# Two 64-token tiles, one batch's loads and a table of conversion steps moved in a fused attention and MLP kernel

## The chip, the cores and the metric

The kernel runs on one core of one Trainium2 chip. The metric is the device time of one execution in microseconds (us); for the kernel before, three runs gave 1006.35, 1006.38 and 1009.82 us, a median of 1006.38 us. The profile is of one more execution, on the same core. Engines are named as in the profile: PE is TensorE, DVE is VectorE, ACT is ScalarE, POOL is GpSimd, and SP is the engine whose queue issues the DMAs.

## The reference

Eight batches of eight heads, 576 tokens, head size 64. Keys and values are averaged over groups of 8 tokens, so each query sees 72 keys. The result goes through an MLP with a leaky ReLU.

```python
k_p = k.reshape(B, H, Sp, pool, D).mean(axis=3)        # 576 -> 72 rows
v_p = v.reshape(B, H, Sp, pool, D).mean(axis=3)
scores = scale * np.matmul(q, k_p.transpose(0, 1, 3, 2))
scores = scores - np.max(scores, axis=-1, keepdims=True)
attn = np.exp(scores)
attn = attn / (np.sum(attn, axis=-1, keepdims=True) + 1e-09)
x = np.matmul(attn, v_p)       # then [B*S, 512] = [4608, 512]
h = x @ w_in                   # [4608, 2048]
g = np.maximum(0.01 * h, h)
out = g @ w_out                # [4608, 512]
```

## The kernel before

**The MLP.** The 4608 tokens are cut into nine chunks of 512. Chunk 0 holds tokens 0 to 511 of batch 0, chunk 1 those of batch 1; the last 64 tokens of both batches wait in a tile `x_tail` and become the first 128 tokens of chunk 2. The hidden size of 2048 is cut into 16 slices f of 128. For one chunk and one slice, `m1` multiplies x by `w_in` (12 matmuls of 512 columns, into a tile `ph`; x and the weight are each split into a high and a low part, and three of the four products are made), ACT applies the leaky ReLU and splits off the high part `gh`, DVE makes the low part `gl`, and `m2` multiplies these by `w_out` (12 matmuls into four accumulators). `m2` runs two slices behind `m1`. The order of the (chunk, slice) pairs is a list of runs (L645): first chunk 0 with slices 0 to 7, then chunk 1 with all 16, then chunk 0 with slices 8 to 15, then chunks 2 to 8. The half-finished chunk 0 is stored in DRAM between the first and the third run.

**The weights.** Each slice of `w_in` and `w_out` arrives as raw 64-bit numbers (`stage`, four slices ahead) and is converted into a high and a low 32-bit part in two steps, a head and a tail (`convert`): two ACT and three DVE instructions (L183 to L189), then one ACT and one DVE instruction (L193, L194). There are 32 conversions, so 64 steps, in the order of `steps`; `convert_to(n)` issues all steps below n. A head or a tail of a given conversion is therefore placed by the calls of `convert_to` and by the letter `c` in the string `FIRST`, each of which is one step.

**The attention.** Work of one tile of (at most) 128 tokens is cut into units: `q` (PE transposes of q into `pq`, ACT copy to `qT`), `sa` (scores into `pss` for four heads, DVE maximum L401, ACT exponential L403), `sb` (sum and reciprocal on DVE, normalised `at` on POOL, or on DVE for tiles 2 and 3 of batch 0), `pu` (PE transposes of `at` into `pp`, ACT and DVE split them into `pT_hi`, `pT_lo`, `pT_rem`), and `au` (16 matmuls of the attention with the pooled values into `pa`, two halves per piece, ACT and DVE split the result into `xh` and `xl`, or DVE copies it into `x_tail`, L488). `ku` and `vu` put the pooled keys and values in place; `lk` and `lv` do the pooling, on DVE for most of batch 0 and on POOL for the others. `PIECES` says which tiles share one `au`.

**The order.** On PE the order is the order in which the code issues (`manual_schedule`, L750). On the other engines a scheduler decides, and `order` below lists what it decided. The opening is the string `FIRST`: the attention of batch 0 with 14 conversion steps strewn in. After it, the units of batch 1 (and the string `TAIL_STEPS`) are spread evenly between the halves of `m1` and `m2` of the first run (L806 to L822); those of batches 2 to 7 stand in the later runs. While batch 0 is worked on, PSUM tiles rotate through eight banks (`banks`, L202); from the `/` in `FIRST` on, attention units have two banks in turn.

**Borrowed space.** `spare(f, i, ...)` hands out the space of a converted weight of a late slice f before that weight exists. Raw k and v of batches 0 and 1 (`RAW`, L213), the wide `at` and `e` tiles and the second set of `pT` tiles (`piece_tiles`, L430) live there. A tile that takes over such a place waits until the last reader of the one before is done.

The functions that the change touches and their callers:

Of the kernel before, what the change touches and what calls it, by code (L numbers as in the profile page):

```python
# [10 lines left out]
F32 = mybir.dt.float32  # L11
# [13 lines left out]
def tile_pooled_attention_ffn(  # L25
# [11 lines left out]
    P = 128  # L37
# [19 lines left out]
        [[(0, 128), (128, 128)], [(256, 128), (384, 128)], [(512, 64)]],  # L57
        WHOLE,
        [[(0, 128), (128, 128)], [(256, 128)], [(384, 128), (512, 64)]],
# [4 lines left out]
    FIRST = (  # L64
# [3 lines left out]
    )  # L68
    TAIL_STEPS = "pu40 au20 pu41 au21"
    SPLIT = 8  # L70
# [133 lines left out]
    turn = 0  # L204

    def bank(b, name):
        nonlocal turn
        pool, tag = banks[turn % len(banks)] if b == 0 else banks[0]
        turn += 1
        return pool.tile([P, NK, P], F32, tag=tag, name=name)  # L210


    RAW = {  # L213
        (0, "k0"): (10, 0), (0, "k1"): (10, 1), (0, "v0"): (11, 0), (0, "v1"): (11, 1),
        (0, "krem"): (9, 0), (0, "vrem"): (9, 1),
        (1, "k0"): (4, 0), (1, "k1"): (4, 1), (1, "v0"): (5, 0), (1, "v1"): (5, 1),
    }
# [94 lines left out]
    tiles = [[x for piece in p for x in piece] for p in PIECES]  # L312
    every = [(b, t) for b in range(B) for t in range(len(tiles[b]))]

    def load_q(b, t):
        s0, n = tiles[b][t]
        if b == 0:
            qr = one.tile([P, H, D], F32, tag=f"xh1_{t}" if t < NK else "xl1_0", name=f"q{b}_{t}")
        else:
            qr = two.tile([P, H, D], F32, tag="q", name=f"q{b}_{t}")  # L320
        nc.sync.dma_start(qr[:n], q[b, :, s0 : s0 + n, :].rearrange("h s d -> s h d"))
        return qr

# [106 lines left out]
    def piece_tiles(b, j, g):  # L430
        if b > 0 or g == 0 or j == 2:
            return pT
        return {
            part: spare(10 - n // 2, n % 2, t.shape, F32R, f"pT_{part}{b}_{j}_{g}")
            for n, (part, t) in enumerate(pT.items())
# [20 lines left out]
    def av_unit(b, j, g, pc):  # L456
        s0 = PIECES[b][j][0][0]
        n = sum(n for _, n in PIECES[b][j])
        w = max(n, PMIN) if b > 0 else n
        for i in range(2):  # L460
# [53 lines left out]
    def attention(b):  # L514
# [5 lines left out]
        def loads():  # L520
# [4 lines left out]
            start_v()  # L525
            for t in range(2, 5):
                q_of[b, t] = load_q(b, t)
# [225 lines left out]
    att[0]["loads"]()  # L753
    stage(0)
    stage(1)
    att[1]["loads"]()
    for f in range(2, SPARE):
        stage(f)

    for u in FIRST.split():  # L760
        if u == "c":
            convert_to(stepped + 1)
        elif u == "/":
            del banks[1:]
            turn = 0
        else:
            att[0][u]()
    att[1]["lk"]()
    att[1]["lv"]()
# [28 lines left out]
    for n, (c, fs) in enumerate(runs):  # L798
# [63 lines left out]
```

## Time and profile before

| | before |
|---|---|
| median of three runs | 1006.38 us |
| span of the profiled execution | 1006.5 us |
| PE busy | 954.4 us (95%) |
| DVE busy | 370.1 us (37%) |
| ACT busy | 428.4 us (43%) |
| POOL busy | 177.7 us (18%) |

The span of the profiled execution, from its first to its last instruction, is 1006.5 us, and no other time of that execution is given; it lies 0.1 us from the median. A start time in the rows is counted from the span's start. Matmul ends in the profile are modelled and overlap the next matmul's start, so the time that a matmul costs is read from one start to the next. A wait in brackets behind a row is the idle time of that engine just before the row, and the instruction that ended it.

### The profile page before, as it was taken

The page shows a single profiled execution, that of the slowest core. Times are in us where ns is not written, and L with a number is a line of the kernel's source. Part 1 is how long each engine was busy: PE and PEld are TensorE (multiplying, and loading weights), DVE is VectorE, ACT ScalarE, POOL GpSimd, SP SyncE. Part 2 cuts the span into 40 slices and gives each one's busy share as a digit, 9 for nine tenths or more (in the row PEclk, how much of TensorE's full clock was granted, in tenths as well). Part 3 has the DMA queues.
Part 4 walks back from the last instruction along what each step waited for, and adds up shares of the span by engine and source line. Part 5 has one row for each costly group of instructions (what it writes and reads, how often), then busy time and mean ns, then how long its engine had stood idle before and what let it go on. Part 6 is the DMA issues. An engine that isn't in the chain of part 4 may idle for free.

```text
span 1006.5 us, 12735 instructions
## 1 busy us (share of the span) xinstructions
PE 954.4 (95%) x4536; PEld 779.0 (77%) x4536; DVE 370.1 (37%) x902; ACT 428.4 (43%) x1386; POOL 177.7 (18%) x292
## 2 busy tenths in 40 slices
PE   4478999999999999999999999999999999999998
PEld 3357778878787778878888888788877888788886
DVE  5998639223432322332232333243323332221111
ACT  5678657234433343424353434344433433332121
POOL 3602200401116610133013301230110100000000
PEclk9679999999999999999999999999999999999999
DMA  9954311312034400221022202110100010001001
GB/s 246 268 170 142 94 54 42 93 43 69 1 102 102 105 11 12 63 71 35 6 64 58 58 1 69 37 37 1 58 22 1 11 48 1 1 1 42 0 1 42
DMA packets 65582, 57.44 MB, mean 57 GB/s; under 512 B 39920, under 2 KB 49136, under 8 KB 65520
## 3 DMA queue, kind: packets, MB, share of 16 engines
q1 hardware_dynamic: 64944, 56.11, 19.8%
q8 instruction: 36, 0.59, 0.2%
q10 hardware_dynamic: 576, 0.52, 0.2%
q14 instruction: 26, 0.21, 0.1%
HBM read 46.14 MB, written 10.49 MB: 56 GB/s over the span
## 4 chain that ended last, share of the span: by engine, by line
PE 79%; DVE 7%; ACT 4%; DMA 4%; issue 2%; POOL 2%; SPq 1%; ACTq 0%; DVEq 0%; POOLq 0%
PE ph L661 12%; PE acc L685 12%; PE ph L663 11%; PE ph L662 11%; PE acc L687 11%; PE acc L686 11%; PE pss L393 4%; PE pp L442 2%; PE pq L368 1%; ACT e L403 1%; DVE w_t L186 1%; DMA v0raw<-in_v_dram 1%; DVE w L194 1%; DVE w_t L189 1%; SPq L240 1%
## 5 line engine op out<-in xcount | busy, mean ns | idle before, releaser
L661 PE MATMUL ph<-xh,w 128*128 128x512 f32 x576 | 237.2, 412 | 1.0 <-DVE gl L670 1.0
L685 PE MATMUL acc<-w,gh 128*128 128x512 f32 x576 | 233.1, 405 | 0.0
L663 PE MATMUL ph<-xh,w 128*128 128x512 f32 x576 | 227.5, 395 | 0.0
L662 PE MATMUL ph<-xl,w 128*128 128x512 f32 x576 | 227.1, 394 | 0.0
L687 PE MATMUL acc<-w,gl 128*128 128x512 f32 x576 | 225.5, 391 | 0.0
L686 PE MATMUL acc<-w,gh 128*128 128x512 f32 x576 | 225.2, 391 | 0.0
L670 DVE TENSOR_TENSOR gl<-ph,gh 128x512 fp32r<-128x512 f32 x144 | 99.5, 691 | 264.6 <-ACT gh L669 263.8
L666 ACT ACTIVATE ph<-ph 128x512 f32<-128x512 f32 x144 | 84.2, 585 | 253.2 <-PE ph L663 253.0
L403 ACT ACTIVATE e<-pss,red 128x72 f32<-128x72 f32 (+1 forms) x320 | 98.2, 320 | 116.9 <-DVE red L401 116.6
L417 POOL TENSOR_TENSOR at<-e,red 128x256 f32<-128x256 f32 (+1 forms) x76 | 47.5, 624 | 543.5 <-DVE red L415 294.7
L663 PEld LDWEIGHTS ph<-xh,w 128*128 128x128 f32 x576 | 109.3, 190 | 24.3
L661 PEld LDWEIGHTS ph<-xh,w 128*128 128x128 f32 x576 | 109.4, 190 | 23.3 <-DVE gl L670 1.5
L687 PEld LDWEIGHTS acc<-w,gl 128*128 128x128 f32 x576 | 108.3, 188 | 23.9
L685 PEld LDWEIGHTS acc<-w,gh 128*128 128x128 f32 x576 | 108.2, 188 | 22.0 <-issue 1.6
L662 PEld LDWEIGHTS ph<-xl,w 128*128 128x128 f32 x576 | 109.7, 190 | 19.2
L686 PEld LDWEIGHTS acc<-w,gh 128*128 128x128 f32 x576 | 108.4, 188 | 19.6
L669 ACT CAST gh<-ph 128x512 fp32r<-128x512 f32 x144 | 85.4, 593 | 3.1
L401 DVE TENSOR_REDUCE red<-pss 128x4 f32<-128x288 f32 (+1 forms) x80 | 36.1, 454 | 95.2 <-PE pss L393 94.3
L403 ACT ACTIVATION_READ_ACCUMULATOR e<-pss,red 128x1 f32 (+1 forms) x320 | 65.4, 204 | 0.0
L393 PEld LDWEIGHTS pss<-kT,qT 128*128 128x128 f32 (+1 forms) x320 | 47.9, 186 | 15.3 <-ACT qT L370 5.8
L393 PE MATMUL pss<-kT,qT 128*128 128x144 f32 (+1 forms) x320 | 54.7, 298 | 4.5 <-ACT qT L370 4.5
L448 DVE TENSOR_TENSOR pT_lo<-pp,pT_hi 128x256 fp32r<-128x256 f32 (+1 forms) x80 | 31.7, 396 | 68.1 <-ACT pT_rem L445 67.5
(95 smaller groups left out, 840.9 us busy)
## 6 DMA issues: line engine op xcount, KB each, us to landing
q<-in_q_dram SPq DMA_DIRECT2D x32, 256.0 KB, 4.3
w_bits<-in_moe_w_in_dram SPq DMA_DIRECT2D x16, 512.0 KB, 3.7
w_bits<-in_moe_w_out_dram SPq DMA_DIRECT2D x16, 512.0 KB, 3.3
out_dram<-o SPq DMA_DIRECT2D x31, 256.0 KB, 2.7
k0raw<-in_k_dram SPq DMA_DIRECT2D x16, 256.0 KB, 3.6
k1raw<-in_k_dram SPq DMA_DIRECT2D x16, 256.0 KB, 4.3
v0raw<-in_v_dram SPq DMA_DIRECT2D x16, 256.0 KB, 4.2
v1raw<-in_v_dram SPq DMA_DIRECT2D x16, 256.0 KB, 5.2
```

The lines of the kernel that those rows point to most:

```text
L393: nc.tensor.matmul(sc[:n, 2 * SP * i : 2 * SP * (i + 1)], qT[:, p, :n], kT[:, p, :, :].rearrange("d i s -> d (i s)"), start=True, stop=True,)
L403: ins = nc.scalar.activation(e[:n, h, :], scv[:n, h, :], AF.Exp, bias=mx[:n, h : h + 1], accum_out=sm[:n, h : h + 1],)
L417: eng.tensor_tensor(at[:n, 0:2, :].rearrange("a i (h s) -> a (i h) s", h=2), e[:n, :, 0:MAIN], sm[:n].unsqueeze(2).broadcast_to([n, 4, MAI ...
L661: nc.tensor.matmul(ph, w[:, 0, ks], xh[kk], start=kk == 0, stop=False)
L662: nc.tensor.matmul(ph, w[:, 0, ks], xl[kk], start=False, stop=False)
L663: nc.tensor.matmul(ph, w[:, 1, ks], xh[kk], start=False, stop=kk == NK - 1)
L666: nc.scalar.activation(ph, ph, AF.Prelu, alpha=0.01)
L669: casts.append(nc.scalar.copy(gh, ph))
L670: nc.vector.tensor_tensor(gl, ph, gh.bitcast(F32), op=ALU.subtract)
L685: nc.tensor.matmul(a, gh[:, r], hi, start=first, stop=False)
L686: nc.tensor.matmul(a, gh[:, r], lo, start=False, stop=False)
L687: nc.tensor.matmul(a, gl[:, r], hi, start=False, stop=last)
```

## The change

The diff, cut to its core:

```diff
     PIECES = [
         [[(0, 128), (128, 128)], [(256, 128), (384, 128)], [(512, 64)]],
-        WHOLE,
+        [[(0, 128), (128, 128)], [(256, 128), (384, 128)], [(512, 64)]],
...
     FIRST = (
-        "lk ku q0 q1 sa00 sb00 sa01 sb01 lv sa10 sb10 sa11 sb11 q2 sa20 sa21 vu pu00 pu10 c c q3 "
-        "pu01 pu11 c sb20 sb21 au00 sa30 sa31 c au01 c pu20 pu21 sb30 sb31 c c pu30 pu31 c au10 au11 "
-        "c q4 c c / sa40 sa41 sb40 sb41 c c c"
+        "lk ku q0 q1 sa00 sb00 sa01 sb01 lv sa10 sb10 sa11 sb11 q2 sa20 sa21 vu pu00 pu10 q3 "
+        "pu01 pu11 sb20 sb21 au00 sa30 sa31 c c au01 pu20 pu21 sb30 sb31 pu30 pu31 c au10 au11 c c"
     )
-    TAIL_STEPS = "pu40 au20 pu41 au21"
+    TAILS = (
+        "0q4 0sa40 0sa41 1q4 0sb40 0sb41 1sa40 1sa41 0pu40 0au20 0pu41 0au21 "
+        "1sb40 1sb41 1pu40 1au20 1pu41 1au21"
+    )
...
+    first_v = spare(11, 0, [P, 2, NK, 2, D], F32R, "v_first")
+    first = (
+        spare(11, 1, [P, NK, 2, SP], F32, "kT_first"), first_v[:, 0], first_v[:, 1],
+        spare(10, 0, [P, 2, 4, D], F32R, "v_rem_first"),
+    )
+    nc.gpsimd.memset(first[0], 0.0)
+    nc.gpsimd.memset(first_v.bitcast(F32), 0.0)
+
+    def keys_values(b):
+        return first if b == 0 else (kT, v_hi, v_lo, v_rem)
...
-        (0, "k0"): (10, 0), (0, "k1"): (10, 1), (0, "v0"): (11, 0), (0, "v1"): (11, 1),
+        (0, "k0"): (4, 0), (0, "k1"): (4, 1), (0, "v0"): (5, 0), (0, "v1"): (5, 1),
         (0, "krem"): (9, 0), (0, "vrem"): (9, 1),
-        (1, "k0"): (4, 0), (1, "k1"): (4, 1), (1, "v0"): (5, 0), (1, "v1"): (5, 1),
+        (1, "k0"): (9, 0), (1, "k1"): (9, 1), (1, "v0"): (10, 1), (1, "v1"): (8, 0),
...
-            part: spare(10 - n // 2, n % 2, t.shape, F32R, f"pT_{part}{b}_{j}_{g}")
+            part: spare(9 + n // 2, (n + n // 2) % 2, t.shape, F32R, f"pT_{part}{b}_{j}_{g}")
...
-        w = max(n, PMIN) if b > 0 else n
+        w = max(n, PMIN) if b > 1 else n
...
     att[0]["loads"]()
-    stage(0)
-    stage(1)
-    att[1]["loads"]()
-    for f in range(2, SPARE):
+    for f in range(SPARE):
         stage(f)
...
+    del banks[1:]
+    turn = 0
+    att[1]["loads"]()
     att[1]["lk"]()
     att[1]["lv"]()
...
-        if n == 0:
-            us = [att[0][u] for u in TAIL_STEPS.split()] + us
+        if n == 1:
+            us = [att[int(u[0])][u[1:]] for u in TAILS.split()] + us
...
-        beats, done, beat = 4 * len(fs), 0, 0
+        beats, done, beat = (24 if n == 1 else 4 * len(fs)), 0, 0
         for f in fs:
             if n == 0:
-                convert_to(14 + 2.8 * f)
+                convert_to(6 + 4 * f)
             elif n == 1:
-                convert_to(36 + 3 * f)
+                convert_to(36 + 2.2 * f)
```

In words: the 64-token tiles of batches 0 and 1 (tile 4) leave the opening and the first run and stand in the second run, spread over its first 20 beats; a beat is half of an `m1` or `m2`. Batch 0 gets its own place for pooled keys and values, so that they are still there then. `FIRST` holds 5 conversion steps in place of 14. The loads of k and v of batch 1 are issued after `FIRST`, into places that batch 0's attention uses until its end. The q tiles of the two small tiles are loaded later as well.

On PE, around the first product (`ph_0` is the first `m1`, `pk` and `pkr` hold the transposed pooled keys of batch 1, `pa_1_3` is the last attention product of batch 0's tiles 0 to 3). Before:

```order
L470 MATMUL pa_1_3_546<-pT_rem_1_1_475,v_rem 128x256
L368 MATMUL pq_4_559<-ident,q_4_148 128x64 x4
L393 MATMUL pss_4_0_577<-kT,qT_4_564 64x144 x2
L393 MATMUL pss_4_1_587<-kT,qT_4_564 64x144 x2
L661 MATMUL ph_0_645<-xh_0_402,w_0_344 128x512
```

Of the change:

```order
L488 MATMUL pa_1_3_502<-pT_rem_1_1_445,v_rem_first 128x256
L679 MATMUL ph_0_567<-xh_0_371,w_0_407 128x512
L680 MATMUL ph_0_567<-xl_0_375,w_0_407 128x512
L681 MATMUL ph_0_567<-xh_0_371,w_0_407 128x512
L679 MATMUL ph_0_567<-xh_1_372,w_0_407 128x512
L680 MATMUL ph_0_567<-xl_1_376,w_0_407 128x512
L681 MATMUL ph_0_567<-xh_1_372,w_0_407 128x512
L342 MATMUL pk_574<-ident,ksum_522 128x128 x4
L346 MATMUL pkr_581<-ident,kremsum_523 128x64
```

The small tile's `pq` and `pss` are gone from here, and `pk` of batch 1, which stood behind two whole `m1`, stands in the middle of the first.

On SP, whose queue issues the DMAs in this order, around batch 1's k and v; the brackets name the engines and the earlier DMAs that an issue waits for. Before:

```order
L165 DMA w_bits_156<-in_moe_w_out_dram 128x1024 [waits DMAHW2_49]
L240 DMA k0raw_162<-in_k_dram 64x2x512 [waits DMAHW3_49]
L240 DMA k0raw_162<-in_k_dram 64x2x512 [waits DMAHW4_49]
L240 DMA k1raw_165<-in_k_dram 64x2x512 [waits DMAHW5_49]
L240 DMA k1raw_165<-in_k_dram 64x2x512 [waits DMAHW6_49]
```

Of the change:

```order
L253 DMA v1raw_537<-in_v_dram 64x2x512 [waits DMAHW3_49]
L163 DMA w_bits_518<-in_moe_w_in_dram 128x4x256 [waits DMAHW4_49,DVE_49,Activation_49]
L163 DMA w_bits_1686<-in_moe_w_in_dram 128x4x256 [waits DMAHW5_49,DMAHW0_49,Pool_49]
L167 DMA w_bits_1688<-in_moe_w_out_dram 128x1024 [waits DMAHW6_49,DMAHW1_49,Pool_49]
L167 DMA w_bits_520<-in_moe_w_out_dram 128x1024 [waits DMAHW7_49,DVE_49,Activation_49]
L253 DMA k1raw_529<-in_k_dram 64x2x512 [waits DVE_49,PE_49]
L253 DMA k0raw_526<-in_k_dram 64x2x512 [waits PE_49,Activation_49]
L253 DMA k0raw_526<-in_k_dram 64x2x512 [waits DMAHW2_49]
L253 DMA k1raw_529<-in_k_dram 64x2x512 [waits DMAHW3_49]
L253 DMA v0raw_534<-in_v_dram 64x2x512 [waits DMAHW4_49,DVE_49,PE_49]
```

Batch 1's k, which waited for nothing but earlier transfers, now waits for PE (the last matmul that reads the second set of `pT` tiles, whose place it takes) and stands behind four weight loads.

On DVE, in the opening (`pT_lo`, `pT_rem` and `xl` belong to the attention of batch 0, `w_t` and `w` to the conversions). Before:

```order
L452 SCALAR_TENSOR_TENSOR pT_rem<-pp_1_0_336,marks,pT_rem 128x128
L185 TENSOR_SCALAR w_t_345<-w_bits_150 128x512
L185 TENSOR_SCALAR w_t_352<-w_bits_152 128x512
L186 SCALAR_TENSOR_TENSOR w_t_345<-w_bits_150,w_t_345 128x512
L186 SCALAR_TENSOR_TENSOR w_t_352<-w_bits_152,w_t_352 128x512
L189 ISA w_t_345<-w_bits_150,w_t_345 128x1024
L448 TENSOR_TENSOR pT_lo_0_1_368<-pp_0_1_370,pT_hi_0_1_367 128x2x128
```

Of the change:

```order
L469 SCALAR_TENSOR_TENSOR pT_rem<-pp_1_0_321,marks,pT_rem 128x128
L465 TENSOR_TENSOR pT_lo_0_1_339<-pp_0_1_341,pT_hi_0_1_338 128x2x128
L469 SCALAR_TENSOR_TENSOR pT_rem_0_1_340<-pp_0_1_341,marks,pT_rem_0_1_340 128x128
L465 TENSOR_TENSOR pT_lo_0_1_339<-pp_1_1_349,pT_hi_0_1_338 128x2x128
L469 SCALAR_TENSOR_TENSOR pT_rem_0_1_340<-pp_1_1_349,marks,pT_rem_0_1_340 128x128
L503 TENSOR_TENSOR xl_0_375<-pa_0_0_366,xh_0_371 128x256
L503 TENSOR_TENSOR xl_1_376<-pa_0_1_381,xh_1_372 128x256
```

The first conversions no longer stand between the attention instructions here; they start 16 rows further down, behind the normalisation of tile 3.

## Rows read from the trace of the kernel before

**Rows 1.** The page, part 2: the span in 40 equal slices of 25.2 us; busy tenths of PE, and the granted PE clock in tenths of full speed (9 and above is the level of 2.4 GHz, 5 that of 1.2 GHz).

```profile
PE   4478999999999999999999999999999999999998
PEclk9679999999999999999999999999999999999999
```

**Rows 2.** Busy time by stretch. Columns: stretch in us, its length, then busy us and instructions of PE, PE's weight loads, DVE, ACT and POOL, then the granted clock, the DMA share and GB/s. The stretches end at the first matmul of batch 0's values stage, at the end of its attention without the small tile, at the first product, at the third `m1`, at the first product of the second run, at the end of that run, and at the end.

```profile
0.00:22.30 22.30, 8.75 (x42) 7.01 (x42) 11.72 (x40) 9.88 (x44) 8.96 (x22) 0.96 0.93 245
22.30:50.61 28.31, 13.87 (x74) 11.60 (x74) 27.98 (x59) 20.13 (x73) 15.52 (x18) 0.68 0.98 268
50.61:52.77 2.16, 1.70 (x13) 1.33 (x13) 2.16 (x7) 0.75 (x2) 0.00 (x0) 0.90 0.84 339
52.77:73.50 20.73, 14.53 (x57) 11.13 (x56) 18.67 (x43) 16.81 (x47) 2.45 (x4) 0.75 0.46 139
73.50:134.17 60.67, 53.15 (x270) 42.06 (x268) 42.91 (x106) 44.76 (x154) 11.37 (x20) 0.97 0.38 111
134.17:222.00 87.83, 86.78 (x384) 71.56 (x383) 41.46 (x79) 39.96 (x76) 13.75 (x18) 1.00 0.22 64
222.00:1006.50 784.50, 775.59 (x3710) 634.29 (x3708) 225.21 (x572) 296.10 (x993) 125.62 (x210) 1.00 0.13 36
```

**Rows 3.** Timeline of PE in the opening: start, length (us), engine, line, operation, tiles, shape, count, and in brackets the wait before it.

```profile
33.05 0.38 PE L468 MATMUL pa<-pT_lo,v_hi 128*128 128x256 f32 x1 [3.46 <-DVE pT_lo L448]
...
43.29 0.90 PE L442 MATMUL pp<-ident,at 128*128 128x128 f32 x3 [7.79 <-DVE at L417]
...
50.17 0.41 PE L470 MATMUL pa<-pT_rem,v_rem 128*128 128x256 f32 x1
50.51 0.67 PE L368 MATMUL pq<-ident,q 64*128 64x64 f32 x4
...
52.77 0.50 PE L661 MATMUL ph<-xh,w 128*128 128x512 f32 x1
```

**Rows 4.** Timeline of DVE in the opening, same columns.

```profile
27.50 2.36 DVE L186 SCALAR_TENSOR_TENSOR w_t<-w_bits,w_t 128x512 int32<-128x512 int32 x2
29.78 1.21 DVE L189 CUSTOM_DVE_ANT_0 w_t<-w_bits,w_t 128x1024 uint16<-128x1024 uint16 x1
...
34.57 2.45 DVE L194 TENSOR_TENSOR w<-w_t,w 128x512 fp32r<-128x512 f32 x2
36.94 4.12 DVE L414 TENSOR_SCALAR red<-red 128x4 f32<-128x4 f32 x1
...
48.33 0.41 DVE L185 TENSOR_SCALAR w_t<-w_bits 128x512 int32<-128x512 int32 x1
48.67 0.68 DVE L189 CUSTOM_DVE_ANT_0 w_t<-w_bits,w_t 128x1024 uint16<-128x1024 uint16 x1
49.27 0.68 DVE L194 TENSOR_TENSOR w<-w_t,w 128x512 fp32r<-128x512 f32 x1
```

**Rows 5.** Timeline of POOL, same columns: the first and the last instruction of the pooling of batch 1's k and v (18 in all), and two of batch 2's.

```profile
27.69 2.75 POOL L228 TENSOR_TENSOR k0raw<-k0raw 128x512 f32<-128x512 f32 x2 [5.48 <-DMA k0raw<-in_k_dram]
...
42.91 0.49 POOL L234 TENSOR_TENSOR vremsum<-vremraw 64x64 f32<-64x64 f32 x1
...
179.67 2.48 POOL L228 TENSOR_TENSOR k0raw<-k0raw 128x512 f32<-128x512 f32 x2 [53.98 <-DMA k0raw<-in_k_dram]
182.23 0.73 POOL L234 TENSOR_TENSOR ksum<-k0raw 128x256 f32<-128x256 f32 x1
183.70 1.29 POOL L228 TENSOR_TENSOR k1raw<-k1raw 128x512 f32<-128x512 f32 x1 [0.73 <-DMA k1raw<-in_k_dram]
```

**Rows 6.** Timeline of SP's queue: the two issues of batch 1's first half of k.

```profile
17.36 1.25 SPq L240 DMA_DIRECT2D k0raw<-in_k_dram  x2
```

**Rows 7.** The chain that ended last, in order of time: the transfer of batch 2's k, alone on the queues.

```profile
175.54 3.97 DMA k0raw<-in_k_dram
```

**Rows 8.** Timeline of PE from the first product to the third `m1`.

```profile
57.17 0.63 PE L442 MATMUL pp<-ident,at 64*128 64x64 f32 x3 [2.74 <-POOL at L417]
...
63.92 0.37 PE L442 MATMUL pp<-ident,at 64*128 64x64 f32 x3 [1.25 <-DVE x_tail L488]
...
70.83 0.94 PE L327 MATMUL pk<-ident,ksum 128*128 128x128 f32 x4
...
73.50 0.47 PE L661 MATMUL ph<-xh,w 128*128 128x512 f32 x1
```

**Rows 9.** Waits of PE from 73.5 to 134.17 us: who waited for whom, us in total, times, longest.

```profile
PE pq L368 <- ACT e L403: 2.6, 2, 2.1
PE pp L442 <- DVE x_tail L488: 1.8, 1, 1.8
```

**Rows 10.** Timeline of PE: pieces of the two small tiles.

```profile
62.06 0.28 PE L467 MATMUL pa<-pT_hi,v_hi 128*128 128x64 f32 x1
...
62.39 0.28 PE L470 MATMUL pa<-pT_rem,v_rem 128*128 128x64 f32 x1
...
111.34 0.46 PE L368 MATMUL pq<-ident,q 64*128 64x64 f32 x4 [2.09 <-ACT e L403]
...
116.79 0.70 PE L393 MATMUL pss<-kT,qT 128*64 128x144 f32 x4
117.42 0.50 PE L685 MATMUL acc<-w,gh 128*128 128x512 f32 x1
...
123.36 0.37 PE L442 MATMUL pp<-ident,at 64*128 64x64 f32 x3 [0.31 <-DVE pT_rem L452]
123.66 0.50 PE L661 MATMUL ph<-xh,w 128*128 128x512 f32 x1
```

**Rows 11.** Timeline of ACT: the four instructions of two conversion heads end where the second row starts.

```profile
62.09 0.70 ACT L183 ACTIVATE w_bits<-w_bits 128x512 f32<-128x512 f32 x1
...
64.32 0.62 ACT L193 CAST w<-w_t 128x512 fp32r<-128x512 f32 x1
```

More of the change, by code (lines that the diff above doesn't have):

```diff
@@ L312, in tile_pooled_attention_ffn @@
     tiles = [[x for piece in p for x in piece] for p in PIECES]
-    every = [(b, t) for b in range(B) for t in range(len(tiles[b]))]
+    every = [(b, t) for b in range(2) for t in range(4)] + [(0, 4), (1, 4)]
+    every += [(b, t) for b in range(2, B) for t in range(len(tiles[b]))]
     def load_q(b, t):
         s0, n = tiles[b][t]
-        if b == 0:
-            qr = one.tile([P, H, D], F32, tag=f"xh1_{t}" if t < NK else "xl1_0", name=f"q{b}_{t}")
+        if b == 0 and t < NK:
+            qr = one.tile([P, H, D], F32, tag=f"xh1_{t}", name=f"q{b}_{t}")
         else:
@@ L324, in place_k @@
     def place_k(b, sums, rem):
+        kT = keys_values(b)[0]
         pk = bank(b, f"pk{b}")
@@ L338, in place_v @@
     def place_v(b, sums, rem):
+        _, v_hi, v_lo, v_rem = keys_values(b)
         for i in range(2):
@@ L388, in s_unit @@
         n = tiles[b][t][1]
+        kT = keys_values(b)[0]
         pss = bank(b, f"pss{b}_{t}_{g}")
@@ L458, in av_unit @@
         n = sum(n for _, n in PIECES[b][j])
-        w = max(n, PMIN) if b > 0 else n
+        w = max(n, PMIN) if b > 1 else n
+        _, v_hi, v_lo, v_rem = keys_values(b)
         for i in range(2):
@@ L525, in loads @@
             start_v()
-            for t in range(2, 5):
+            for t in range(2, NK):
                 q_of[b, t] = load_q(b, t)
@@ L762, in tile_pooled_attention_ffn @@
             convert_to(stepped + 1)
-        elif u == "/":
-            del banks[1:]
-            turn = 0
         else:
             att[0][u]()
+    del banks[1:]
+    turn = 0
+    att[1]["loads"]()
     att[1]["lk"]()
```

## The prediction

> **What bounds the kernel now.** I read the page's slices first, then busy time by stretch, then the timelines of the first 140 us, and last the waits of PE. The slices show PE at nine tenths or more from the fourth slice on, and a granted clock below full only in the first three [rows 1]. The stretches say where the time that can be saved lies. The second run takes 87.83 us for 384 matmuls, 0.229 us each at the full clock with nothing between them, and the 784 us behind it are 99% busy [rows 2]. Whatever is added there is paid in full. Before the second run, at 134.17 us, PE is not full: 14 of 28 us in the opening's second part, 14.5 of 20.7 us around the first two `m1`, 53 of 61 us in the rest of the first run [rows 2]. In the opening DVE is the bound: busy 27.98 of 28.31 us [rows 2], and PE's long waits there, 3.46 and 7.79 us, end on DVE [rows 3]. After 73.5 us no engine is full: PE 53, DVE 43 and ACT 45 of 61 us [rows 2]; what is lost goes into short waits from engine to engine, 2.6 and 1.8 us the largest [rows 9].
>
> So the sum has two sides: how much earlier the second run begins than at 134.17 us, and how much longer it gets. Durations come from an execution of 1006.5 us, 0.1 us above the median of the three runs, so no correction is made.
>
> **The opening: from 50.5 us to about 44.** Between the first conversion and the last split of `pT` (48.3 us) DVE did 4 instructions of L185, 4 of L186, 3 of L189 and 2 of L194; of the change two each of the first three and none of L194. From start to start L185 takes 0.34 us, L189 0.60 us [rows 4], and I take 0.60 for the other two, which are listed with similar lengths when nothing disturbs them. Removed: 2 x 0.34 + 5 x 0.60 = 3.7 us. Second, DVE was slowed while POOL pooled batch 1 (27.69 to 43.4 us [rows 5]): L186 took 2.36 us for two, L189 1.21, L194 2.45 for two, and a tiny L414 4.12 us [rows 4]. Against 0.68 apiece and about 0.2 for the small one this is 1.0 + 0.5 + 1.1 + 3.9 = 6.5 us. Of POOL's 18 instructions nine (both remainders and half of v) still fall into the opening, the shorter ones; I leave 2.5 us of the 6.5, which removes 4. New is that DVE waits for the exponentials of tile 3, 1 to 2 us that conversions used to fill. 48.3 - 3.7 - 4 + 1.5 = 42.1, and the last eight `pa` matmuls follow at half clock (0.21 us each, as at 50.17 us [rows 3]): 44. Bounds: 41 if POOL disturbs nothing, 48.5 if it disturbs as much as before.
>
> The weights' transfers move ahead of batch 1's; I cost that at nothing, since the first conversion now starts later, at some 32 us. The extra memsets on POOL stand in its idle time before 12 us.
>
> **The new wait: batch 1's keys.** Before, they were pooled while DVE held the opening up anyway, and PE took them at 70.83 us without a wait [rows 8]. Now their transfer can be issued only when the last `pa` has read the `pT` tiles, at 44 us. Four issues of 0.6 us [rows 6], the first landing 4 us after its issue when alone on the queues [rows 7], and I take 4.5 with the weight loads ahead of it; then POOL's adds until the second half of the sum: three long ones at 1.3 to 1.7 us and five at 0.74 us [rows 5], 7.9 us. So `pk` starts at 44 + 0.7 + 4.5 + 7.9 = 57 us. In between PE does half an `m1`: `xl` is ready at 47 to 48 us, six matmuls at half clock (0.43 us) take 2.6 us, and PE then waits about 7 us. Queued behind it are the second half of `m1`, and through it everything of the first run. DVE and ACT go on converting meanwhile, DVE disturbed by the pooling.
>
> Behind `pk` comes ACT: the copy `qT` for batch 1's first tile stands behind a conversion tail that waits for DVE. DVE has some 20 instructions (10.9 us) from 47.5 us to there, plus 3.8 us of disturbance: 62.2; then tail, `gh`, four head instructions in 2.23 us [rows 11] and the copy: 66 us. The third `m1` starts at about 67.5 us, against 73.50 [rows 8]: 6 us gained, half of which is the small tile's units and the two waits behind them, 2.74 and 1.25 us [rows 8].
>
> A rule of the Trainium skill speaks against this wait. The trace shows it first: behind the 7.79 us wait [rows 3] the granted clock of that part of the opening is 0.68 on average, and 0.75 around the first `m1` [rows 2]. The page "TensorE: Matmul & The Clock Gate", section "HAM oscillation — how this bites in real kernels", says that a PE that idles between bursts is throttled again and starts each burst at half rate. By that rule the 18 matmuls behind `pk` cost 0.43 us instead of 0.23, 3.6 us more. In my sum it costs nothing up to 66 us, since the copy on ACT comes later either way; the trace agrees with the rule but makes it matter only for the slower rival.
>
> **The rest of the first run: from 60.7 us to 54.5.** Taken out: batch 1's small tile. From rows at full clock [rows 10]: `pq` 0.4, two `pss` of 0.63, two `pp` of 0.30, and its 64 columns in sixteen wide `pa` 0.5: 2.8 us; and one `pss` of 0.4 now lies earlier. Its two waits (2.09 before `pq`, 1.8 behind the `x_tail` copies [rows 9, 10]) go with it. Added: `pss` of tile 2 now stands directly ahead of `pa`, which needs its PSUM bank, and ACT reaches that exponential only behind four head instructions: about 3 us. Conversions: the change arrives with three conversions (6.5 us of DVE) fewer done, but without the small tiles' work; DVE and ACT each have about 45 us of work in 54, as full as PE. 60.7 - 2.8 - 0.4 - 3.9 + 3 = 56.6, less 2 us of half clock that followed the 2.09 us wait: 54.5. Bounds: 50 (as full as PE was at 90 to 108 us) and 60 (nothing saved but the small tile).
>
> The second run then starts at 67.5 + 54.5 = 122 us: 12.2 us earlier.
>
> **The second run: 9.2 us longer.** Both small tiles now stand where PE is full. Each costs 0.4 + 2 x 0.63 + 2 x 0.30 + 16 x 0.11 = 4.0 us [rows 10], since batch 1's own `pa` no longer shares columns: 8.0 us. The beats leave six matmuls or 1.4 us between a unit and the one that needs it; ACT and DVE queue their own work there, so I add 1.2 us of short waits (bounds 0 and 4). Fewer conversion steps per slice (2.2 for 3) cost nothing: all 64 are issued by slice 13, and DVE is busy 41 of 88 us [rows 2].
>
> **Sum:** 1006.5 - 12.2 + 9.2 = 1003.5; I say 1003 us.
>
> **Rivals.**
> The first run flows. If POOL hardly disturbs DVE and the conversions keep ahead, `pk` comes at 54 and the second run at 116 us: 1006.5 - 18.2 + 9 = 997.5. For it: all three engines then have slack of 10 us each. Against it: DVE was 99% busy in the opening, and no stretch before 134 us ran that full on PE.
>
> The keys come late. The transfers of k stand behind four weight loads of 512 KB, some of which are issued only when DVE and POOL are through; if those are still moving, k lands after 52 us, POOL and DVE disturb each other for longer, and `pk` comes at 64 us. PE then takes the 18 matmuls at half clock (3.6 us), ACT's copy is no cover any more, the third `m1` starts at 75 us, and the second run at 130: 1006.5 - 4.2 + 9.5 = 1012. It decides from `pk` later than about 61 us: there the gain before the second run falls under the 9 us added to it. For it: the queues move 268 GB/s with a share of 0.98 up to 50 us [rows 2]. Against it: a load needs 4 us alone.
>
> The work only changes place. The gain before the second run is eaten by the new wait, and the small tiles cost what they cost before: 1006.5. For it: PE must do all of this work anyway, plus sixteen matmuls.
>
> **How the numbers follow.** This kernel's runs tell 0.5%, 5 us, from no change. Forecast (1003, own range 999 to 1007): 0.47, of which a quarter lies below 1001.4. Free flow (994 to 1001): 0.27. No gain: 0.06. Late keys (1009 to 1017): 0.20, two thirds of it above 1011.4. Faster: 0.27 + 0.12 = 0.39; slower: 0.13; same: the rest, 0.48. The range that holds 8 in 10 takes in most of the free flow and the start of the late keys: 995 to 1010.
>
> **What would show it.** In the changed profile: no instruction of 4 us on DVE before 42 us; the first product at 46 to 48 us; a wait of about 7 us of PE for `ksum` in its middle; the third `m1` at 66 to 69 us; the second run's first matmul at 120 to 124 us; 8 to 10 us more between it and the third run's. It would be wrong if `pk` waits beyond 61 us, if PE in the first run waits for weights instead of ACT and DVE, or if the small tiles hold PE up for more than 4 us in the second run.

## The result, and the profile after

The changed kernel takes 1013.39 us (median of four runs, 1012.12 to 1015.22), the kernel before 1006.37 us beside it: a ratio of 1.0067, 95% interval 1.0048 to 1.0086. It is slower by 7 us. The forecast was 1003 us with a range of 995 to 1010; the time lies above it, and to a time above 1011.4 us the prediction had given 0.13. Of four runs of a later repeat (e8 below) the one that was profiled took 1096.15 us at a granted clock of 0.837, and the ratio and the median of e8 leave it out.

The profiled execution of the change has a span of 1011.4 us, 4.9 us more than before, and took 1013.22 us: 1.8 us lie around the span. The prediction took the span of before, 1006.5 us, for a time; with the same 1.8 us (1.7 to 1.9 in every run whose span and time are both known) that execution took some 1008.3 us (an estimate), 2 us over its median. So profile against profile shows 4.9 us and the medians 7.0.

The page's slices after, for [rows 1]:

```profile
PE   4547999999999999999999999999999999999998
PEclk9769999999999999999999999999999999999999
```

The third and fourth slices, 50.6 to 101.1 us, lost a part: PE was at 7 and 8 tenths there and is at 4 and 7. Busy time by stretch, for [rows 2], cut at the end of batch 0's attention, at the third `m1`, at the second run's first product, and at `pk` of batch 2, which stands at the same place of the third run in both kernels (columns as in [rows 2]). Before, for the last two stretches:

```profile
134.17:226.64 92.47, 91.42 (x404) 75.33 (x403) 41.49 (x79) 41.10 (x78) 13.75 (x18) 1.00 0.20 60
226.64:1006.50 779.86, 770.95 (x3689) 630.52 (x3687) 225.18 (x571) 294.96 (x992) 125.62 (x210) 1.00 0.13 36
```

After:

```profile
22.60:45.01 22.41, 13.58 (x73) 12.29 (x73) 20.70 (x52) 20.88 (x75) 6.76 (x10) 0.66 0.69 225
45.01:74.45 29.44, 11.73 (x39) 7.69 (x38) 19.95 (x41) 10.46 (x26) 13.56 (x9) 0.65 0.63 187
74.45:129.20 54.75, 48.20 (x245) 39.62 (x244) 40.99 (x96) 42.17 (x134) 10.09 (x16) 0.97 0.41 124
129.20:230.94 101.74, 101.74 (x472) 81.65 (x471) 49.13 (x105) 49.30 (x123) 21.07 (x26) 1.00 0.21 60
230.94:1011.40 780.46, 770.85 (x3689) 630.50 (x3687) 224.71 (x571) 294.62 (x992) 125.28 (x210) 1.00 0.13 36
```

The second run begins 134.17 - 129.20 = 4.97 us earlier, takes 101.74 - 92.47 = 9.27 us longer, and the rest 0.60 us: 4.9 in sum. The stretch that stands out is the second one: 29.44 us in which PE works 11.73 and ACT 10.46. The timeline of PE (columns as in [rows 3], with which it compares, and [rows 8]) shows where:

```profile
44.90 0.28 PE L488 MATMUL pa<-pT_rem,v_rem_first 128*128 128x256 f32 x1
45.01 0.42 PE L679 MATMUL ph<-xh,w 128*128 128x512 f32 x1
48.34 0.79 PE L680 MATMUL ph<-xl,w 128*128 128x512 f32 x1 [2.90 <-DVE xl L503]
...
62.89 0.69 PE L342 MATMUL pk<-ident,ksum 128*128 128x128 f32 x2 [12.05 <-POOL ksum L247]
64.25 0.69 PE L342 MATMUL pk<-ident,ksum 128*128 128x128 f32 x2 [0.68 <-POOL ksum L247]
...
74.45 0.40 PE L679 MATMUL ph<-xh,w 128*128 128x512 f32 x1
...
98.81 0.39 PE L485 MATMUL pa<-pT_hi,v_hi 128*128 128x256 f32 x1 [3.61 <-ACT e L420]
```

Half an `m1` is done by 50.6 us, and PE then waits 12.05 us for the pooled keys. The timeline of POOL, for [rows 5], says why:

```profile
51.05 7.31 POOL L241 TENSOR_TENSOR k0raw<-k0raw 128x512 f32<-128x512 f32 x1 [11.80 <-DVE w_t L188]
58.32 1.25 POOL L241 TENSOR_TENSOR k1raw<-k1raw 128x512 f32<-128x512 f32 x1
...
63.48 0.72 POOL L247 TENSOR_TENSOR ksum<-k1raw 128x256 f32<-128x256 f32 x1
```

The same add takes 7.31 us on k0 and 1.25 us on k1. DVE meanwhile (timeline, for [rows 4]):

```profile
51.34 0.41 DVE L187 TENSOR_SCALAR w_t<-w_bits 128x512 int32<-128x512 int32 x1
51.67 0.68 DVE L191 CUSTOM_DVE_ANT_0 w_t<-w_bits,w_t 128x1024 uint16<-128x1024 uint16 x1
...
56.56 0.68 DVE L188 SCALAR_TENSOR_TENSOR w_t<-w_bits,w_t 128x512 int32<-128x512 int32 x1
65.09 0.87 DVE L358 SCALAR_TENSOR_TENSOR v_lo<-vsum,v_hi 64x256 fp32r<-64x256 f32 x2 [7.86 <-ACT v_hi L357]
```

From 51.34 to 57.24 us DVE runs eleven conversion instructions with no gap, each at its undisturbed length (0.68 us for L191, against 1.21 beside POOL's adds in [rows 4]). The add ends at 58.36, 1.1 us after DVE falls idle. Then DVE stands still for 7.86 us: the next in its queue is the placing of v, which waits for ACT's copy, and that for POOL's sum of v (timeline of ACT):

```profile
64.64 0.85 ACT L357 ACTIVATE v_hi<-vsum 64x256 fp32r<-64x256 f32 x2 [8.90 <-POOL vsum L247]
...
68.13 0.58 ACT L684 ACTIVATE ph<-ph 128x512 f32<-128x512 f32 x1 [1.63 <-PE ph L681]
```

So one add that made no headway holds up PE, ACT and DVE together.

### The profile page after: what moved, and what is told of

It is laid out like the page before. It is cut to its first block, busy times and chain, and to the rows that moved or that the text cites. A ratio compares the mean times of both kernels' runs of the same rounds, so it can differ in the third digit from the quotient of the medians.

```text
span 1011.4 us, 12771 instructions
## 1 busy us (share of the span) xinstructions
PE 955.0 (94%) x4552; PEld 778.9 (77%) x4552; DVE 368.3 (36%) x902; ACT 427.2 (42%) x1386; POOL 187.0 (18%) x294
## 4 chain that ended last, share of the span: by engine, by line
PE 88%; ACT 4%; DMA 2%; issue 2%; DVE 2%; POOL 1%; SPq 1%; ACTq 0%; POOLq 0%; DVEq 0%
PE acc L703 13%; PE ph L679 13%; PE acc L705 13%; PE acc L704 13%; PE ph L681 12%; PE ph L680 12%; PE pss L410 4%; PE pp L459 3%; PE pq L384 1%; ACT e L420 1%; SPq L253 1%; PE pa L486 1%; PE pa L488 1%; PE pa L487 1%; PE pa L485 1%
## 5 line engine op out<-in xcount | busy, mean ns | idle before, releaser
L434 POOL TENSOR_TENSOR at<-e,red 128x256 f32<-128x256 f32 (+1 forms) x76 | 51.5, 677 | 537.1 <-DVE red L432 281.9
L410 PEld LDWEIGHTS pss<-kT,qT 128*128 128x128 f32 (+1 forms) x280 | 41.1, 180 | 12.7 <-ACT qT L386 3.4
L410 PE MATMUL pss<-kT,qT 128*128 128x144 f32 (+1 forms) x280 | 46.9, 290 | 2.8 <-ACT qT L386 2.8
```

What stands on the lines that cost most here:

```text
L410: nc.tensor.matmul(sc[:n, 2 * SP * i : 2 * SP * (i + 1)], qT[:, p, :n], kT[:, p, :, :].rearrange("d i s -> d (i s)"), start=True, stop=True,)
L434: eng.tensor_tensor(at[:n, 0:2, :].rearrange("a i (h s) -> a (i h) s", h=2), e[:n, :, 0:MAIN], sm[:n].unsqueeze(2).broadcast_to([n, 4, MAI ...
```

## The experiments

Theory A: GpSimd's add is held up by VectorE's gapless conversions. Rivals: B, the keys' transfers are late; C, ACT and DVE stand behind the placing of v, so that early keys alone bring little. All ratios are to the kernel before, measured beside the run. The kernel before gave medians of 1005.44 to 1007.87 us beside the experiments, so the times below compare by their ratios and not as they stand. One table first, of the profiled executions, in us; "second run" is its first product, "length" goes from there to `pk` of batch 2:

| run | time | ratio (95%) | last `pa` from | third `m1` | second run | length |
|---|---|---|---|---|---|---|
| before | 1006.37 | | 50.17 | 73.50 | 134.17 | 92.47 |
| changed | 1013.39 | 1.0067 (1.0048 to 1.0086) | 44.90 | 74.45 | 129.20 | 101.74 |
| e1 | 1008.95 | 1.0022 (1.0006 to 1.0037) | 44.54 | 66.42 | 125.80 | 101.71 |
| e2 | 1014.65 | 1.0059 (1.0036 to 1.0083) | 42.67 | 71.06 | 130.77 | 101.72 |
| e3 | 1005.90 | 0.9975 (0.9962 to 0.9988) | 42.81 | 65.06 | 121.86 | 101.75 |
| e4 | 1007.44 | 0.9997 (0.9984 to 1.0009) | 43.62 | 63.06 | 122.91 | 101.96 |
| e5 | 1003.38 | 0.9974 (0.9963 to 0.9985) | 42.68 | 65.18 | 121.07 | 101.75 |
| e6 | 1013.14 | 1.0068 (1.0049 to 1.0087) | 44.59 | 71.97 | 129.19 | 101.76 |
| e7 | 1004.71 | 0.9990 (0.9978 to 1.0002) | 43.24 | 66.62 | 128.24 | 96.48 |
| e9 | 997.26 | 0.9915 (0.9901 to 0.9929) | 42.81 | 59.72 | 114.65 | 101.76 |
| e10 | 1006.30 | 0.9993 (0.9981 to 1.0005) | 42.94 | 59.38 | 122.95 | 101.71 |
| e11 | 1005.47 | 0.9979 (0.9964 to 0.9993) | 50.58 | 73.88 | 133.15 | 91.21 |
| e12 | 1003.60 | 0.9959 (0.9943 to 0.9974) | 47.38 | 60.50 | 120.98 | 101.71 |

**e1: VectorE idle while GpSimd pools.**

```diff
+            keys = anchor.get("keys")
+            with tc.issue_after(keys.ins) if keys else nullcontext():
+                nc.vector.tensor_scalar(t, high, -0x80000000, None, op0=ALU.bitwise_and)
...
+        taken = nc.vector.tensor_scalar_mul(kT[64:128, :, 1, 0:MAIN], pk[64:128, :, 64:128], KSCALE)
+        if b == 1:
+            anchor["keys"] = taken
```

> The changed kernel, with the VectorE part of every conversion step behind the first six queued behind VectorE's copy of `pk`, so that VectorE has nothing to do while GpSimd pools batch 1's k. Same transfers, same adds on GpSimd. Theory A (GpSimd's adds are held up by VectorE's gapless conversions): the first add of k0raw takes 1.3 to 1.7 us instead of 7.31, pk starts at 57 to 59 us instead of 62.9, and the conversions, about 6 us of VectorE work, come later instead, so that the second run starts no more than 2 us earlier than at 129.2: 1010 to 1015 us. Theory B (the keys' transfers are late, and the row begins before its data is there): the first add still ends at 57 us or later, pk at 62 us or later, 1014 to 1020 us.

POOL and DVE of e1, timelines:

```profile
50.75 1.26 POOL L243 TENSOR_TENSOR k0raw<-k0raw 128x512 f32<-128x512 f32 x1 [10.95 <-DMA k0raw<-in_k_dram]
51.97 1.26 POOL L243 TENSOR_TENSOR k1raw<-k1raw 128x512 f32<-128x512 f32 x1
...
57.13 0.72 POOL L249 TENSOR_TENSOR ksum<-k1raw 128x256 f32<-128x256 f32 x1
```

```profile
48.83 1.27 DVE L198 TENSOR_TENSOR w<-w_t,w 128x512 fp32r<-128x512 f32 x2
58.74 0.87 DVE L362 SCALAR_TENSOR_TENSOR v_lo<-vsum,v_hi 64x256 fp32r<-64x256 f32 x2 [8.64 <-ACT v_hi L361]
```

With DVE empty the add takes 1.26 us and `pk` begins at 56.54 us. Only the place of DVE's conversions was changed, and k0 landed at about the same time (50.5 us against 50.8 in the changed kernel): A is shown and B falls. The time was better than expected: the second run begins 3.4 us earlier, not 2 at most. Of the 8 us won at the third `m1` the first run gives 4.6 back (59.38 us against 54.75), since DVE does the held conversions there.

**e2 and e3: the pooling on VectorE**, of k alone, then of k and v.

```diff
-        eng = nc.vector if b == 0 else nc.gpsimd      # load_k; in e3 load_v too
+        eng = nc.vector if b < 2 else nc.gpsimd
...
-            pooled(nc.gpsimd, sums[:, 0:2], raws[0], P)                                  # e3
+            pooled(nc.vector if b == 1 else nc.gpsimd, sums[:, 0:2], raws[0], P)
```

> The changed kernel with batch 1's k pooled on VectorE, in its queue among the conversions; v stays on GpSimd. Theory A: the nine adds cost VectorE 4 us, none of them takes over 1 us, and pk starts at 54 to 57 us. GpSimd's add of v0raw may still be held up, and ACT's copies of v with it. Theory C (ACT and VectorE stand behind the placing of v, whose sum GpSimd makes, so an early pk alone brings little): pk at 54 to 57 us but the third m1 not before 72 us, second run at 127 to 130, 1010 to 1014 us; without C the third m1 at 67 to 69 us, second run at 122 to 125, 1005 to 1009 us. Theory B: pk not before 60 us.

> The changed kernel with batch 1's k and v both pooled on VectorE (GpSimd pools nothing of batch 1). Theory A with C: pk at 54 to 58 us and no wait of ACT for vsum beyond 60 us, third m1 at 67 to 70 us, second run at 122 to 126 us, 1005 to 1010 us. Theory B: pk not before 60 us, third m1 after 72 us, 1012 us or more.

POOL and DVE in e2:

```profile
54.22 4.03 POOL L241 TENSOR_TENSOR v0raw<-v0raw 128x512 f32<-128x512 f32 x2 [12.66 <-DVE k0raw L241]
55.91 0.42 DVE L247 TENSOR_TENSOR ksum<-k0raw 128x256 f32<-128x256 f32 x1
59.26 0.87 DVE L358 SCALAR_TENSOR_TENSOR v_lo<-vsum,v_hi 64x256 fp32r<-64x256 f32 x2 [2.93 <-ACT v_hi L357]
...
60.76 0.42 DVE L247 TENSOR_TENSOR ksum<-k1raw 128x256 f32<-128x256 f32 x1
```

In e2 the first half of ksum is there at 56.3 us, but the placing of v stands between the halves in DVE's queue, and v's two adds, still on POOL, take 4.03 us instead of 2.0; the first of them, 3.23 us, again ends 1.1 us after DVE falls idle (56.33 us). The second `pk` comes at 61.24 us and the third `m1` at 71.06, and the second run begins 1.6 us later than in the changed kernel: C holds too, although the first run also takes 5 us longer, which C alone does not explain. In e3 nothing waits for POOL (PE's wait for ksum, 9.5 us, is now for DVE's adds), the second run begins 7.3 us earlier than in the changed kernel, and the kernel passes the one before.

**e4: the loads early again.**

```diff
-        (1, "k0"): (9, 0), (1, "k1"): (9, 1), (1, "v0"): (10, 1), (1, "v1"): (8, 0),
+        (1, "v0"): (3, 0), (1, "v1"): (3, 1),
...
+        if b == 1 and nm in ("krem", "vrem"):
+            tag = "xl1_0" if nm == "krem" else "xl1_1"
+            return one.tile([P, 1, POOL * D], F32, tag=tag, name=f"{nm}raw{b}")
```

> The changed kernel with batch 1's k and v loaded into places that are free from the start (k in the two buffers of the tag raw, the remainders in xl1_0 and xl1_1, v in the places of the fourth slice's weights), so the loads wait for no matmul; the rest as in the changed kernel. If the later loading is what made the change slower: no wait of PE for ksum, third m1 at 62 to 67 us, second run at 117 to 122 us, still 101.7 us from there to the third run: 999 to 1004 us. Rival (the pooling, back in the opening, slows VectorE there as it did before): the last pa ends at 48 us or later instead of 44.7, an instruction of 2 us or more on VectorE before 44 us, third m1 at 67 to 70 us, 1004 to 1008 us.

```profile
42.16 3.41 DVE L187 TENSOR_SCALAR w_t<-w_bits 128x512 int32<-128x512 int32 x1
```

The wait for ksum is gone and the third `m1` at 63.06 us, as expected, but now POOL has the run and DVE is held: an L187 of 0.41 us takes 3.41, and `xl` behind it comes only at 52.1 us (PE waits 6.9 us). POOL's adds run without a gap from 42.21 to 51.17 us. The last `pa` was not later, so the rival was right about the mechanism and not about its place; the time, 1007.44 us, is the rival's, but early loads alone bring the changed kernel level with the one before.

**e5: `pa` ahead of tile 2's `pss`** (on e3), to remove the wait of 3.61 us above (3.8 in e3).

```diff
-                if nxt and nxt[0] == b and (nxt[0], nxt[2]) not in fresh:
+                late = b == 1
+                if not late and nxt and nxt[0] == b and (nxt[0], nxt[2]) not in fresh:
                     add(b, f"sa{nxt[2]}0")
...
                 add(b, f"au{j}0")
+                if late and nxt and nxt[0] == b and (nxt[0], nxt[2]) not in fresh:
+                    add(b, f"sa{nxt[2]}0")
+                    fresh[nxt[0], nxt[2]] = 1
```

> Run e3 (batch 1's k and v pooled on VectorE) with one unit of TensorE's order moved: the `pss` of batch 1's tile 2 stands behind the first pair of `pa` instead of directly ahead of it, so that `pa` no longer needs the PSUM bank that ACT's exponential still reads. Theory: the wait of 3.8 us before `pa` goes and with it some 2 us of half clock behind it; second run at 117 to 119 us instead of 121.9, 1000 to 1003 us. Rival (ACT and VectorE, busy 45 of 57 us, are the bound of the first run, so the wait turns up again before a later `pss`, `pq` or `pa`): second run at 121 to 122 us, 1005 to 1007 us.

```profile
90.67 0.76 PE L410 MATMUL pss<-kT,qT 128*128 128x144 f32 x4 [2.90 <-DVE xl L503]
```

The wait moved to the `pss`: 2.90 us for DVE. The ratio is that of e3; the rival was right.

**e6 and e12: nine conversion steps back ahead of the first product**, on e3 and on e9.

```diff
-        "... vu pu00 pu10 q3 pu01 pu11 sb20 sb21 au00 sa30 sa31 c c au01 pu20 ... c au10 au11 c c"
+        "... vu pu00 pu10 c c q3 pu01 pu11 c sb20 sb21 au00 sa30 sa31 c au01 c pu20 ... c c c c c c"
```

> Run e3 with the nine conversion steps back ahead of the first product, where they stood before the change. By the prediction's price (3.7 us of VectorE for them in the opening, the rest of the gain from less pooling on GpSimd) the last `pa` ends at 46 to 47.5 us instead of 43.2. Rival (the steps cost more than their own time there, and the pooling cost little): it ends at 49 us or later. The first run gets back what was done ahead: third m1 at 66 to 69 us, second run at 121 to 125 us, 1004 to 1009 us.

> Run e9 with the nine conversion steps back ahead of the first product. In e6 they cost 7 us, and the row of k0raw there shows VectorE idle for 3.42 us until k landed. If it was that the weight loads, issued earlier, stood ahead of k: with k loaded early the steps cost only their own time on VectorE, 2 to 4 us in the opening, and are got back in the first run: second run at 114 to 117 us, 996 to 1000 us. Rival (VectorE is the bound and the steps lie in front of the last splits of pT): last `pa` ends at 46 us or later, second run at 119 to 123 us, 1002 to 1006 us.

```profile
55.45 0.69 DVE L241 TENSOR_TENSOR k0raw<-k0raw 128x512 f32<-128x512 f32 x1 [3.42 <-DMA k0raw<-in_k_dram]
```

In e6 the last `pa` starts 1.8 us later than in e3, less than either side expected, but the first add of k0 starts 5.45 us later (50.00 there), DVE waits for the transfer in this row, and the third `m1` comes at 71.97 us, where 66 to 69 was expected. Here the keys are late, as the prediction's rival said of the changed kernel. The likely reason is that earlier conversions free the raw weights' places earlier, so that weight loads go out close ahead of k and between its parts, as SP's queue in e6 shows:

```profile
42.83 0.37 SPq L163 DMA_DIRECT2D w_bits<-in_moe_w_in_dram  x1
44.02 0.34 SPq L167 DMA_DIRECT2D w_bits<-in_moe_w_out_dram  x1
44.60 0.61 SPq L253 DMA_DIRECT2D k1raw<-in_k_dram  x1
45.32 0.60 SPq L253 DMA_DIRECT2D k0raw<-in_k_dram  x1
46.01 0.55 SPq L163 DMA_DIRECT2D w_bits<-in_moe_w_in_dram  x1
```

In e12, with k early, the last `pa` starts 4.6 us later than in e9 and the second run 6.3 us; the rival's numbers came, and DVE is busy 24.74 of 25.20 us from 22.30 to 47.50 us, so it is the bound there. So moving the nine steps behind the first product was a gain, not the loss (tried with the pooling on DVE alone).

**e7: batch 1's small tile back in the first run** (on e3).

```diff
-        [[(0, 128), (128, 128)], [(256, 128), (384, 128)], [(512, 64)]],      # batch 1
+        WHOLE,
...
-        "0q4 0sa40 0sa41 1q4 0sb40 0sb41 1sa40 1sa41 0pu40 0au20 0pu41 0au21 "
-        "1sb40 1sb41 1pu40 1au20 1pu41 1au21"
+        "0q4 0sa40 0sa41 0sb40 0sb41 0pu40 0au20 0pu41 0au21"
...
-    every = [(b, t) for b in range(2) for t in range(4)] + [(0, 4), (1, 4)]
+    every = [(b, t) for b in range(2) for t in range(4 + b)] + [(0, 4)]
```

> Run e3 with batch 1's small tile back in the first run; batch 0's stays in the second. The second run gets 4.6 us shorter (97.1 us from its start to the third run's `pk` instead of 101.7). If a tile costs the same wherever TensorE does it, the second run starts 4.6 us later, at 126.5 us, and the time is that of e3, 1005 to 1007 us. Rival (in the first run ACT and VectorE are the bound, so it costs 6 us or more there, and moving it does pay): second run at 128 us or later, 1007 to 1010 us.

The second run starts 6.4 us later and is 5.3 us shorter. In this trace moving the tile is worth 1 us; the intervals of the two ratios overlap, so the times do not tell it from nothing.

**e8: the changed kernel once more** gave 1011.50 us (median of 1010.88, 1011.50 and 1013.50), ratio 1.0058 (1.0038 to 1.0077).

> The changed kernel once more, beside the same runs of before as the experiments: 1011 to 1015 us, ratio 1.004 to 1.008, and again an add of k0raw on GpSimd of over 5 us that ends about 1 us after VectorE goes idle.

```profile
51.25 7.24 POOL L241 TENSOR_TENSOR k0raw<-k0raw 128x512 f32<-128x512 f32 x1 [12.73 <-DMA k0raw<-in_k_dram]
```

The long add is there again, and ends 1.1 us after DVE falls idle (57.37 us).

**e9: early loads, pooling on VectorE, `pa` first** (e4, e3 and e5 together).

> Runs e4 and e5 together: batch 1's k and v loaded early into free places, and pooled on VectorE; `pa` ahead of tile 2's `pss`. Theory: the wait of 10 us for ksum that e3 and e5 still have goes, since the keys' transfer no longer waits for the last `pa`; but VectorE's 8 us of pooling now lie in the opening, where it is the bound, so the last `pa` ends at 45 to 47 us instead of 43 and the first product is late by as much. pk at 50 to 53 us, third m1 at 59 to 62 us instead of 65.2, second run at 116 to 119 us instead of 121.1: 1000 to 1002.5 us. Rival (the first run is bound by ACT and VectorE, whose work comes no earlier): third m1 early, second run at 121 us, 1003 to 1005 us.

```profile
42.81 0.28 PE L491 MATMUL pa<-pT_rem,v_rem_first 128*128 128x256 f32 x1
...
49.23 1.05 PE L345 MATMUL pk<-ident,ksum 128*128 128x128 f32 x4
...
59.72 0.39 PE L686 MATMUL ph<-xh,w 128*128 128x512 f32 x1
```

997.26 us: faster than both kernels, and faster than expected. The eight us of pooling did not delay the last `pa` (42.81, as in e3), since DVE does 4 of the 18 adds before and 14 behind the last split of `pT`, and `pk` no longer waits. The second run begins 14.5 us earlier than in the changed kernel.

**e10: the units three beats later** (on e5), so that two whole `m1` stand ahead of `pk`.

```diff
+                    off = 3 if n == 0 else 0
-                    while done < min(len(us), len(us) * beat // (beats - 4)):
+                    while done < min(len(us), len(us) * max(0, beat - off) // (beats - 4 - off)):
```

> Run e5 with batch 1's attention units three beats later in TensorE's order of the first run, so that two whole `m1` (24 matmuls) stand ahead of `pk` instead of six matmuls. Theory: the wait of 10 us for ksum is filled with 5 us of matmuls, the third m1 starts at 62 to 64 us, second run at 117 to 119 us: 999 to 1002 us. Rival (ACT and VectorE are the bound of the first run, and the units closer together wait more): second run at 120 to 123 us, 1003 to 1006 us.

The third `m1`, which now has fewer units ahead of it, begins 5.8 us earlier than in e5 and the second run 1.9 us later. Filling PE's wait brought nothing: in between DVE is busy 51.95 of 63.57 us, and the units, closer together, wait for it and ACT. The rival was right.

**e11: the kernel before, with the pooling on VectorE** (e3's edit on it).

> The kernel before, with nothing changed but that batch 1's k and v are pooled on VectorE instead of GpSimd. GpSimd's disturbance of VectorE (6.5 us by the prediction's rows) goes, 18 adds of 0.3 to 0.7 us, 8 us in all, are added to VectorE, which is the bound of that opening. If the tiles, the conversions and their order made e9 fast: the last `pa` ends at 49 to 53 us, as before or later, second run at 133 to 137 us, 1006 to 1010 us. Rival (sharing the pooling between the engines was all that cost, in both kernels, and the change itself is worth nothing): the last `pa` ends at 46 us or earlier, second run at 128 us or earlier, below 1001 us.

0.9979, some 2 us, for that alone; the last `pa` and the second run (50.58 and 133.15 us) lie where the first theory has them. The ratios of e11, e12 and e9 also say which part of the change pays: 0.9979 with the pooling moved, 0.9959 in e12, which has all of e9 except the later conversions, and 0.9915 in e9. Of e9's 8.5 us some 2 are the pooling and 4.4 the later conversion steps; what is left, some 2 us for the tiles and everything else, is not told from nothing, since the intervals of e11 and e12 overlap.

## Why the prediction was wrong

**The failed step** is in "The new wait": "then POOL's adds until the second half of the sum: three long ones at 1.3 to 1.7 us and five at 0.74 us [rows 5], 7.9 us". It measured 51.05 to 64.20 us, 13.2 us, 5.3 more, because the first add took 7.31 us. The prediction had read [rows 4, 5] as "DVE was slowed while POOL pooled batch 1" and priced the new overlap the same way ("DVE and ACT go on converting meanwhile, DVE disturbed by the pooling", 3.8 us of it). There POOL got through (2.75 us for its first two adds [rows 5], against 1.26 and 0.72 us in e1) and DVE was held, up to 4.12 us in a small L414. In the opening of the changed kernel this still holds (the row under "The opening" below); behind the arrival of k it is the other way round: DVE ran undisturbed, so the 3.8 us did not come, and POOL was held. The rows showed that one of the two engines waits; that it would be the same one in a new order was assumed. The Trainium skill, page "SBUF — State Buffer", section "Who interferes with whom", says that a DVE instruction in a two-port mode, or one with two SBUF inputs beside a GpSimd instruction that reads SBUF, contends for a port pair that the two engines share, and that whichever issues first blocks the other for its whole instruction. The traces agree that either can be the one that blocks (POOL 7.31 us in the changed kernel, DVE 3.41 us in e4). But a wait for one DVE instruction, as the rule has it, would be at most 0.7 us by these rows, and here POOL waited for eleven; the measurement goes further than the page.

**The rest of that step** was near: the last `pa` ended at 45.01 us (said to end at 44), k0 landed at 50.8 (49.2 by the sum), and the second `pk` came at 64.25 against 57. These 7 us went straight on to the third `m1`: 74.45 against 67.5, 6.95 us late. This is the whole error before the second run. Not foreseen was who else stood behind the sum: ACT and DVE, through the placing of v, for 8.90 and 7.86 us (in e2, with k on DVE, this still keeps the second `pk` until 61.24 us).

**The opening.** The last `pa` ended at 45.01 us, inside 41 to 48.5 and 1.0 us off the value. The conversions ahead of the last split of `pT` are the six that the prediction counted; moved back, nine steps cost the last `pa` 1.8 us (e6 against e3) and 4.6 us (e12 against e9), around the 3.7 set down. The waits for tile 3's exponentials came to 1.2 us (1.5). The miss is POOL's remaining disturbance: six DVE instructions between 32.3 and 38.9 us took 3.6 us more in sum than the same ones undisturbed, where 2.5 were left. The longest:

```profile
34.87 2.05 DVE L188 SCALAR_TENSOR_TENSOR w_t<-w_bits,w_t 128x512 int32<-128x512 int32 x1
```

No DVE instruction of 4 us stands before 42 us, as said.

**The first run.** 54.75 us against 54.5, with the wait of 3.61 us at `pa` that was put at 3. Against [rows 2] PE's busy time fell by 4.95 us (5.2 by the sum) and its idle time by 0.97 (0.9), so the terms fit and not only the total. By e5 that wait costs nothing that ACT and DVE would not cost elsewhere.

**The second run.** 9.27 us longer against 9.2. PE has no wait in it (busy 101.74 of 101.74 us), so the 1.2 us set down for short waits did not come. PE's busy time rose by 101.74 - 91.42 = 10.3 us where 8.0 were put. The added matmuls themselves take 7.9 us from start to start; but 24 of the MLP's matmuls that stand beside the added units take 0.31 to 0.34 us instead of 0.23, 2.4 us in sum, a cost that the prediction left out:

```profile
136.25 0.70 PE L410 MATMUL pss<-kT_first,qT 128*64 128x144 f32 x4
136.88 0.50 PE L679 MATMUL ph<-xh,w 128*128 128x512 f32 x1
137.22 0.40 PE L680 MATMUL ph<-xl,w 128*128 128x512 f32 x1
```

And a wait of 1.0 us that stood there before is gone. So 9.2 was right by luck: the misses cancel. (One tile taken back, in e7, makes this run 5.3 us shorter, against the 4.0 set down for one.)

**The rivals.** "The keys come late" named the numbers that came: `pk` at 64, third `m1` at 75, second run at 130, 1012 us; measured 64.25, 74.45, 129.20 and 1013.39. Its cause was only half right. Its condition was k landing after 52 us; k0 landed at 50.8, and e1, with the same transfers, has `pk` at 56.54. Its other half, that POOL and DVE disturb each other for longer, was the cause, but had no price of its own. The prediction had also named the sign, `pk` beyond 61 us. The rival had a chance of 0.20, too little for something that [rows 4] showed at 4.12 us in one instruction. "The first run flows" did not come, and e5 and e10 show why: a wait of PE that is taken away there turns up again as a wait for ACT or DVE. The half clock behind the wait was there: the granted clock was 0.65 from 45.01 to 74.45 us, and behind `pk` six of the 18 matmuls took 0.42 to 0.59 us from start to start (65.16 to 67.98 us), 1.4 us in sum over 0.23 apiece; the other twelve were back at about 0.23. "The keys come late" had all 18 slow, 3.6 us, and the forecast let them cost nothing. It was not quite nothing: ACT waits 1.63 us for the `ph` of these six (68.13 us), and the copy `qT`, for which PE waits 2.08 us ahead of the third `m1`, stands behind that.

**Against the median** the forecast was 10 us off: 7 from the keys, 0.6 behind the second run, and 2 (the estimate above) from the profiled execution of before being that much slower than its median.

What stays open is why POOL got in between DVE's conversions before, at 27.69 us [rows 4, 5], and not at 51.05 us after the change: how short a pause of DVE lets it in, and which instructions hold it, was not tried.

## What to carry to other kernels

When two engines slow each other in a trace, do not carry the loss over to the same engine in a new order: price also the case in which the one on the critical path is held until the other pauses. A sum that three engines wait for does not belong on an engine that a stream of filler work on another can hold up; here, moving 18 adds to the busier engine was worth 7 us of start of the second run. And a load that starts early into free space is worth more than one that waits for borrowed space (e9 against e5: 6.4 us).

## What was not expected of the hardware

One GpSimd add of 128 x 512 went from 1.26 to 7.31 us (7.24 in e8) while DVE ran eleven instructions without a gap, at full speed, and it ended 1.1 us after the last, as the held adds of e8 and e2 did: of the 6.2 us before, next to nothing was progress. The reverse is in e4: a DVE instruction of 0.41 us took 3.41 while POOL added without a gap.
